# A new instruction order for an attention and feed-forward kernel: second-half K/Q loads ahead of the weights, scores of steps 2 and 3 ahead of the feed-forward part, copies split over two engines

## Chip, cores and metric

The kernel runs on one core of a Trainium2 chip. The metric is the device time of one execution in microseconds (us), lower is better. The profile's engines are TensorE (PE; PEld is its weight load), VectorE (DVE), ScalarE (ACT), GpSimd (POOL) and SyncE (SP, used here to issue transfers). "Clock" is the mean granted TensorE clock of a run, 1.0 being full speed.

## What is computed

Four batches of eight heads, 768 positions, head dimension 64. In the inputs given, three heads attend causally, the other five only to the first 4 positions and a window of 64. The result goes through a feed-forward part that takes the larger of three products.

```python
scores = np.where(mask, scale * q @ k.T, -1e9)           # mask per head: causal, or first 4 + window
a = np.exp(scores - max); a = a / a.sum(-1)
attn = a @ v                                              # (4, 8, 768, 64)
x = attn.transpose(0, 2, 1, 3).reshape(3072, 512)
h = np.maximum(np.maximum(x @ w1, x @ w2), x @ w3)        # 512 -> 768, three weights
out = h @ w_out                                           # 768 -> 512
```

## The kernel before

The work is 16 *steps* (batch, half of the sequence, quartet of heads) of attention and eight *feed-forward parts* (batch, half). A part needs the turned result xT of two steps. Its work is cut into groups, which a generator hands out one by one between the scores of later steps ("fill"), so that TensorE has something to do while ScalarE takes exponentials.

```python
def load(b, qd):                  # K and Q of four heads of a batch, cast to fp16 on the way
    st = stage.tile([P, 2, S // R, D], FP16, tag="kq", name="kq")
    for i, src in enumerate((k, q)):
        nc.gpsimd.dma_start(out=st[:, i], in_=src[b, G * qd : G * qd + G]...)
# ... cut ...
def ffn(b, half):                 # one feed-forward part, one "yield" a group
    for wi, ni in order:
        yy = psum()
        for ks in range(KS):
            nc.tensor.matmul(yy[:, 0:HALF], w_t[wi][:, ks, ...], xT[b, half][ks]..., ...)
        if wi == 0:
            nc.scalar.copy(out=acc[ni], in_=yy[:, 0:HALF])           # accumulator copy
        else:
            nc.vector.tensor_tensor(out=dst, in0=yy, in1=acc[ni], op=ALU.max)
        yield
# ... cut ...
def av(t, i):                     # attention product of a head pair, scaled, then turned
    # ... matmuls into o, x = o / row sums ...
    if t in BY_DMA:               # steps 2 and 4 to 15: turned by a transposing transfer
        nc.sync.dma_start(out=xT[b, half][hp], in_=x..., transpose=True)
    else:                         # the other steps: turned on TensorE
        xs[t, i] = x
# ... cut: the start, up to the first feed-forward groups ...
PROGRAM = (                       # due groups, whether pairs are apart, four lists of items
    # ... cut ...
    (2.8, False, "", "", "av 4 1", "av 5 0, load 2 0, v 6 0 pp"),
    (3.6, False, "x 5 0", "load 2 1", "", "av 5 1"),
    # ... cut: ten rows ...
    (3.94, False, "", "", "av 9 0, v 9 1 ap", "load 3 0"),
    (3.6, False, "", "x 9 0, load 3 1", "x 9 1", ""),
    # ... cut ...
)
```

`load b qd` loads K and Q of four heads of batch b; `turn` turns them in 32x32 blocks on VectorE; `v` casts values; `masks` (called in the scores) multiplies exponentials by the mask.

The softmax here doesn't subtract the row's maximum and nothing guards it: scores larger than these inputs give would overflow.

Of the kernel before, what the change touches and what calls it, by code (L numbers as in the profile page):

```python
# [38 lines left out]
APART = [(0, 0, 1, (384,), 128, 0), (1, 1, 1, (384,), 128, 0)] + MASKED[1][1:]  # L39

# [11 lines left out]
def kernel(  # L52
# [14 lines left out]
    nc = tc.nc  # L67
# [21 lines left out]
    BY_DMA = (2, 4, 5, 6, 7, 8, 9, 10, 11, 12, 13, 14, 15)  # L89

    consts = ctx.enter_context(tc.tile_pool(name="consts", bufs=1))
    stage = ctx.enter_context(tc.tile_pool(name="stage", bufs=3))
    half16 = ctx.enter_context(tc.tile_pool(name="half16", bufs=3))
# [27 lines left out]
    def load_pairs(half, hp, n, engines, alone=False):  # L121
        for nm, src, eng in zip(("ks", "qs"), (k, q), engines):
            st = stage.tile([P, 4, HB, D], FP32, tag=nm, name=nm)
            m = 2 if alone else 2 * n
            for h in range(0, 2 * n, m):
                eng.dma_start(
                    out=st[:, h : h + m],
                    in_=src[
                        0, 2 * hp + h : 2 * hp + h + m, half * HALF : (half + 1) * HALF
                    ].rearrange("h (p j) d -> p h j d", p=P),  # L130
                )
            for i in range(n):
                staged.setdefault((half, hp + i), []).append(st[:, 2 * i : 2 * i + 2])

# [12 lines left out]
    def turn_pair(half, hp, *engines):  # L147
# [4 lines left out]
        for part, op in enumerate(engines):  # L152
            tr = bank([P, 1024], FP16, "tr")
            for i in range(n):
                for j in range(HB):
                    c = i * HALF + j * P
                    nc.tensor.transpose(  # L157
                        tr[:, c : c + P],
                        xs[part + i][:, j].rearrange("p h d -> p (h d)"),
                        ident,  # L160
                    )
# [34 lines left out]
    after = consts.tile([1, 2], FP16, name="after")  # L196

    def sync_after(x):
        nc.sync.dma_start(out=after, in_=x)
# [3 lines left out]
    def load_v(b, half, engines=None):  # L203
        engines = engines or (nc.sync,) * HB
        vs = stage.tile([P, H, HB, D], FP32, tag="vs", name="vs")
        for j in range(HB):
            r0 = half * HALF + j * P
            engines[j].dma_start(
                out=vs[:, :, j], in_=v[b, :, r0 : r0 + P].rearrange("h p d -> p h d")
            )  # L210
        staged_v[b, half] = vs

    load_pairs(0, 0, 1, (nc.sync, nc.scalar))
    ir32 = consts.tile([1, 2 * H], mybir.dt.int32, name="ir32")
    nc.sync.dma_start(out=ir32, in_=is_retrieval.bitcast(mybir.dt.int32).unsqueeze(0))
    load_pairs(0, 1, 1, (nc.sync, nc.scalar))
    load_pairs(0, 2, 2, (nc.sync, nc.scalar), True)
    load_v(0, 0)


    zero = consts.tile([P, 512], FP16, name="zero")
    nc.vector.memset(zero, 0.0)

# [52 lines left out]
    def head_flags():  # L276
        flags = bank([P, H], FP32, "flags")
        nc.tensor.matmul(flags, base[0:1, 0:P], RT1, start=True, stop=True)
# [26 lines left out]
    def load_weight(wi):  # L305
        if wi < 3:
            nc.gpsimd.dma_start(
                out=w_t[wi],
                in_=(moe_w1, moe_w2, moe_w3)[wi].rearrange("(ks p) n -> p ks n", p=P),
            )  # L310
        else:
            nc.gpsimd.dma_start(
                out=woutt, in_=moe_w_out.rearrange("(ns p) m -> p ns m", p=P)
            )
# [4 lines left out]
    def ffn(b, half):  # L319
# [15 lines left out]
        for wi, ni in order:  # L335
            yy = psum()
            for ks in range(KS):
# [5 lines left out]
                )  # L343
            if wi == 0:
                acc[ni] = accp.tile([P, HALF], FP16, tag="acc", name="acc")
                nc.scalar.copy(out=acc[ni], in_=yy[:, 0:HALF])  # L346
# [6 lines left out]
        for tb in range(HB):  # L353
# [5 lines left out]
            for c, op, eng in (  # L359
                (0, nc.scalar.copy, nc.sync), (n, nc.vector.tensor_copy, nc.scalar),  # L360
# [14 lines left out]
    queue = []  # L375

    def fill(n):
# [28 lines left out]
    def scores(t, u, pairs=(0, 1)):  # L406
# [5 lines left out]
        m = 1 if u == 1 and (t == 0 or t == 1 and pairs == (0,)) else 2  # L412
# [37 lines left out]
        for x, st in sts.items():  # L450
# [5 lines left out]
            if not early:  # L456
                masks(t, i, u)


    MASK_ON_DVE = ((2, 0, 1), (3, 0, 0), (3, 0, 1), (3, 1, 3), (5, 0, 0), (5, 1, 0), (5, 1, 1), (7, 0, 1))  # L460

    def masks(t, i, u):
# [3 lines left out]
        for at, u0, nu, cols, n, m0 in APART if t in (3,) else MASKED[half]:  # L466
# [11 lines left out]
            engine = nc.vector if (t, i, u) in MASK_ON_DVE else nc.gpsimd  # L478
# [4 lines left out]
    def av(t, i):  # L483
# [29 lines left out]
        if t in BY_DMA:  # L513
# [6 lines left out]
    def turn_x(t, i, op=None):  # L520
        b, half, qd = where(t)
        hp = 2 * qd + i
        if t not in BY_DMA:
# [10 lines left out]
        if hp == NHP - 1:  # L534
# [4 lines left out]
    cast_pair(0, 0, (act, act))  # L539
    idle_work(8)  # L540
    read_flags()
    idle_work(2)
    head_flags()
    turn_pair(0, 0, dve, act)
    head_masks(0, True)
    cast_pair(0, 1, (pool, act))
    turn_pair(0, 1, dve)
    cast_pair(0, 2, (pool, pool))
    scores(0, 0, (0,))
    scores(0, 1, (0,))  # L550
    head_masks(1, True)
    load_weight(0)
    scores(0, 0, (1,))
    far_flags()
    cast_pair(0, 3, (pool, pool))
    head_masks(3, True)
    head_masks(2, True)
    turn_pair(0, 2, dve)
    scores(0, 1, (1,))
    turn_pair(0, 3, dve)  # L560
    prep_v(0, 0, dve, nc.gpsimd)
    prep_v(1, 0, dve, nc.vector)
    load_pairs(1, 0, 2, (nc.gpsimd, nc.gpsimd))
    prep_v(1, 1, pool, nc.gpsimd)
    scores(1, 0, (0,))
    scores(1, 1, (0,))
    scores(1, 0, (1,))
    prep_v(0, 1, act, nc.vector)
    av(0, 0)
    scores(1, 1, (1,))  # L570
    av(1, 0)
    av(0, 1)
    turn_x(0, 0, act)
    av(1, 1)
    load_weight(1)
    turn_x(0, 1, act)
    head_masks(0)
    cast_pair(1, 1, (act, act))
    load_pairs(1, 2, 2, (nc.gpsimd, nc.gpsimd))
    load_weight(2)  # L580
    load_v(0, 1, (nc.gpsimd,) * HB)
    turn_x(1, 0, dve)
    turn_x(1, 1, dve)
    cast_pair(1, 0, (act, act))
    fill(4)
    head_masks(2)
    turn_pair(1, 1, dve)
    turn_pair(1, 0, dve)
    head_masks(3)
    load_weight(3)  # L590
    fill(1)
    fill(1)
    fill(1)
    head_masks(1)






    FIRST = 4
    PROGRAM = (
        (2.4, True, "", "", "cast 1 2 dp", ""),
        (2.4, False, "load 1 0", "", "cast 1 3 da", ""),
        (2.0, False, "", "pair 1 2", "load 1 1", ""),
        (2.2, False, "pair 1 3", "v 2 0 ap", "", "v 2 1 ap"),
        (2.2, False, "", "gate, load_v 1 0", "", ""),
        (1.6, True, "", "av 2 0", "", "turn 1 0 0 0"),
        (1.0, True, "turn 1 0 0 1", "", "av 2 1, turn 1 0 1 0", ""),
        (2.2, True, "turn 1 0 1 1, load_v 1 1", "", "v 3 1 pp, v 3 0 ap, x 2 0", "turn 1 1 0 0"),  # L610
        (3.6, False, "turn 1 1 0 1", "x 2 1", "turn 1 1 1 1, av 3 1", ""),
        (2.8, False, "v 4 0 pp, av 3 0", "turn 1 1 1 0", "v 4 1 ap", ""),
        (3.6, False, "x 3 0, x 3 1", "", "", ""),
        (3.6, False, "av 4 0", "", "x 4 0, v 5 1 pp", "x 4 1, v 5 0 ap"),
        (2.8, False, "", "", "av 4 1", "av 5 0, load 2 0, v 6 0 pp"),
        (3.6, False, "x 5 0", "load 2 1", "", "av 5 1"),
        (3.8, False, "", "x 5 1", "", ""),
        (2.8, False, "", "load_v 2 0", "turn 2 0 1 0", "v 6 1 ap"),
        (4.8, False, "turn 2 0 0 1", "", "turn 2 0 0 0", "av 6 0"),
        (4.2, False, "", "", "", "x 6 0, x 6 1, turn 2 0 1 1"),  # L620
        (3.4, False, "", "av 6 1", "turn 2 1 0 1", ""),
        (5.4, False, "load_v 2 1", "v 7 0 ap, turn 2 1 0 0", "turn 2 1 1 0", "v 7 1 ap"),
        (3.4, False, "", "turn 2 1 1 1", "v 8 0 ap, x 7 0", "av 7 0"),
        (3.8, False, "av 7 1", "", "", "v 8 1 pp"),
        (3.94, False, "x 7 1", "", "av 8 0", "v 9 0 ap, av 8 1"),
        (3.2, False, "", "x 8 0, x 8 1", "", ""),
        (3.94, False, "", "", "av 9 0, v 9 1 ap", "load 3 0"),
        (3.6, False, "", "x 9 0, load 3 1", "x 9 1", ""),
        (5.6, False, "v 10 0 ap, av 9 1", "v 10 1 ap", "", ""),
        (3.14, False, "", "load_v 3 0", "turn 3 0 1 0", ""),  # L630
        (3.6, False, "turn 3 0 0 1", "av 10 0", "turn 3 0 0 0", ""),
        (3.4, False, "", "x 10 0", "av 10 1", "turn 3 0 1 1"),
        (6.2, False, "", "", "turn 3 1 0 1", "v 11 0 ap"),
        (3.2, False, "load_v 3 1", "turn 3 1 0 0", "turn 3 1 1 0", ""),
        (3.2, False, "v 11 1 pp", "x 10 1, turn 3 1 1 1", "v 12 0 ap", "av 11 0, x 11 0"),
        (3.4, False, "", "av 11 1", "", "v 12 1 ap"),
        (5.0, False, "x 11 1", "", "av 12 0", "v 13 0 ap, av 12 1"),
        (3.2, False, "", "x 12 0, x 12 1", "", ""),
        (4.0, False, "", "", "av 13 0, v 13 1 pp", ""),
        (5.2, False, "", "x 13 0", "x 13 1", ""),  # L640
# [86 lines left out]
```

## Time and profile before

| | before |
|---|---|
| time, median of the runs beside the changed kernel | 200.95 us (200.65 to 201.27, 4 runs); this kernel's runs in the later rounds had clock 0.996 to 1.0 |
| TensorE, VectorE, ScalarE, GpSimd busy | 189.7, 122.5, 131.7, 123.3 us of a span of 199.3 |
| first feed-forward matmul of parts 0, 1, 2, 3 | 17.8, 50.1, 70.9, 94.3 us |
| K/Q loads of batch 2 issued, of batch 3 issued | 56.7 and 62.9 us; 100.3 and 105.5 us |

A second measure is used below: **lost time**. I give every matmul, the idle ones at the start left out, the time that it takes at the steady pace of the same traces (0.163 us for 384 columns, 0.216 us for 512, and so on), which sums to 171.4 us for either kernel, and subtract from the clock of the span the work begun until then. Before, 17.1 us are lost at 50 us, 18.4 at 70, 19.0 at 80 and 24.1 at 190 us. It is my own sum, good to a few tenths; it also sees slow matmuls and small gaps, which the busy columns hide.

### The profile page before, as it was taken

How to read it: one execution, taken by the hardware profiler on the slowest of the kernel's cores; microseconds unless marked ns; L12 is line 12 of the kernel's file. 1: busy time of each engine (PE TensorE's matmuls, PEld its weight loads, DVE VectorE, ACT ScalarE, POOL GpSimd, SP SyncE). 2: the span in 40 equal slices, each digit the busy share in tenths (PEclk: the TensorE clock that was granted, in tenths of full speed). 3: DMA queues.
4: the chain of work that ended last, by engine and by line, in shares of the span. 5: the costliest groups of instructions: out<-in, count | busy, mean ns of one | idle time of the engine just before them, and what ended most of it. 6: DMA issues, size and time to landing. Idle time of an engine off the chain costs nothing.

```text
span 199.3 us, 5133 instructions
## 1 busy us (share of the span) xinstructions
PE 189.7 (95%) x2059; PEld 109.5 (55%) x2059; DVE 122.5 (61%) x241; ACT 131.7 (66%) x206; POOL 123.3 (62%) x154
## 2 busy tenths in 40 slices
PE   7897999996999999999999999999999999999992
PEld 2455555545566465574555565565555565755652
DVE  2698587999687829861555649961555234543540
ACT  4585798786966776676786775848758769323221
POOL 3599159789887906787969635799847447400000
PEclk9999999999999999999999999999999999999999
DMA  6999999994949991904359995513410250023004
GB/s 182 270 213 245 278 238 212 213 202 112 256 81 154 194 274 43 178 0 146 95 101 132 170 254 141 85 26 98 116 23 20 105 76 20 3 64 135 3 0 158
DMA packets 43245, 26.48 MB, mean 133 GB/s; under 512 B 33558, under 2 KB 38230, under 8 KB 43222
## 3 DMA queue, kind: packets, MB, share of 16 engines
q1 hardware_dynamic: 37206, 15.01, 34.9%
q0 software_dynamic: 4784, 10.23, 26.7%
q10 hardware_dynamic: 1232, 0.92, 1.5%
q8 instruction: 16, 0.26, 0.6%
q14 instruction: 7, 0.06, 0.1%
HBM read 25.17 MB, written 6.29 MB: 158 GB/s over the span
## 4 chain that ended last, share of the span: by engine, by line
PE 78%; DVE 8%; ACT 4%; DMA 3%; issue 3%; POOL 2%; SPq 1%; ACTq 0%; POOLq 0%; DVEq 0%
PE yy L338 43%; PE yy L364 12%; PE st L441 10%; PE oacc L495 8%; DVE KQ L190 4%; PE yst L338 3%; ACT pt L452 3%; DMA ks<-in_k_dram 2%; DVE x L505 2%; DMA out_dram<-ot 1%; PE tr L157 1%; PE yst L364 1%; POOL kn L139 1%; DVE hT L349 1%; POOL qn L139 0%
## 5 line engine op out<-in xcount | busy, mean ns | idle before, releaser
L479 POOL TENSOR_TENSOR pt<-pt,mk 128x512 f16<-128x512 f16 (+1 forms) x76 | 80.6, 1084 | 34.8 <-ACT pt L452 34.7
L452 ACT ACTIVATE pt<-st 128x1024 f16<-128x1024 f32 (+3 forms) x99 | 83.1, 894 | 19.4 <-PE st L441 18.6
L349 DVE TENSOR_TENSOR acc<-yy,acc 128x384 f16<-128x384 f32 x45 | 25.1, 558 | 28.9 <-PE yy L338 19.3
L338 PE MATMUL yy<-xT,w1t 128*128 128x384 f16 x180 | 36.1, 327 | 0.1
L338 PE MATMUL yy<-xT,w0t 128*128 128x384 f16 x180 | 35.6, 326 | 0.4 <-DVE xT L531 0.4
L338 PE MATMUL yy<-xT,w2t 128*128 128x384 f16 x180 | 35.7, 327 | 0.0
L346 ACT CAST acc<-yy 128x384 f16<-128x384 f32 x45 | 21.0, 485 | 17.0 <-PE yy L338 10.5
L364 PE MATMUL yy<-woutt,hT 128*128 128x512 f16 (+1 forms) x138 | 32.0, 375 | 0.0
L441 PE MATMUL st<-KQ 32*128 32x384 f16 (+4 forms) x560 | 28.7, 279 | 1.0 <-DVE KQ L190 0.8
L349 DVE TENSOR_TENSOR hT<-yy,acc 128x384 f16<-128x384 f32 x45 | 25.1, 560 | 6.6 <-PE yy L338 4.0
L495 PEld LDWEIGHTS <-pt 128*128 128x128 f16 x672 | 24.0, 97 | 5.3 <-issue 2.1
L190 DVE STREAM_TRANSPOSE KQ<-kq 128x384 f32<-128x384 f32 x24 | 25.7, 1130 | 0.0
L338 PEld LDWEIGHTS <-w0t 128*128 128x128 f16 x192 | 18.2, 98 | 12.9 <-issue 1.0
L495 PE MATMUL oacc<-va,pt 128*128 128x65 f16 x352 | 24.8, 193 | 0.3 <-ACT va L392 0.3
L338 PEld LDWEIGHTS <-w2t 128*128 128x128 f16 x192 | 17.6, 98 | 13.3 <-issue 2.1
L338 PEld LDWEIGHTS <-w1t 128*128 128x128 f16 x192 | 17.2, 98 | 12.8 <-issue 1.3
L370 ACT COPY ot<-yy 128x512 f32<-128x512 f32 x22 | 12.9, 588 | 15.9 <-PE yy L364 9.6
L364 PEld LDWEIGHTS <-hT 128*128 128x128 f16 x150 | 14.0, 98 | 14.6 <-issue 0.3
L441 PEld LDWEIGHTS <-KQ 32*128 32x128 f16 (+1 forms) x560 | 12.2, 93 | 17.8 <-issue 11.5
L495 PE MATMUL oacc<-vf,pt 128*128 128x65 f16 x320 | 21.2, 193 | 0.8 <-POOL vf L394 0.8
L505 DVE TENSOR_TENSOR x<-oacc,rc 128x384 f16<-128x384 f32 x32 | 17.8, 557 | 1.1
L503 DVE RECIPROCAL rc<-oacc 128x6 f32<-128x6 f32 x32 | 6.1, 192 | 20.0 <-PE oacc L495 19.8
(70 smaller groups left out, 129.9 us busy)
## 6 DMA issues: line engine op xcount, KB each, us to landing
out_dram<-ot SPq DMA_DIRECT2D x23, 256.0 KB, 3.1
vs<-in_v_dram SPq DMA_DIRECT2D x21, 256.0 KB, 6.3
kq<-in_k_dram POOLq DMA_DIRECT2D x6, 384.0 KB, 5.6
kq<-in_q_dram POOLq DMA_DIRECT2D x6, 384.0 KB, 8.0
qs<-in_q_dram ACTq DMA_DIRECT2D x4, 192.0 KB, 4.0
ks<-in_k_dram SPq DMA_DIRECT2D x4, 192.0 KB, 3.6
w0t<-in_moe_w_dram POOLq DMA_DIRECT2D x1, 768.0 KB, 7.4
ks<-in_k_dram POOLq DMA_DIRECT2D x2, 384.0 KB, 7.2
```

What stands on the lines that cost most here:

```text
L190: nc.vector.transpose(out=dst.rearrange("c (p j) -> c j p", j=n)[:, j0:j1], in_=src.rearrange("c (j i) -> c j i", i=R),)
L338: nc.tensor.matmul(yy[:, 0:HALF], w_t[wi][:, ks, ni * P : (ni + 1) * P], xT[b, half][ks].rearrange("p a t -> p (a t)"), start=(ks == 0), s ...
L346: nc.scalar.copy(out=acc[ni], in_=yy[:, 0:HALF])
L349: nc.vector.tensor_tensor(out=dst, in0=yy[:, 0:HALF], in1=acc[ni], op=ALU.max)
L364: nc.tensor.matmul(yo[:, 0:n], hT[ns][:, tb * P : (tb + 1) * P], woutt[:, ns, c : c + n], start=(ns == 0), stop=(ns == NNB - 1),)
L370: op(out=ot[:, c : c + n], in_=yo[:, 0:n])
L441: nc.tensor.matmul(sts[g // m][:, g % m, c0 : c0 + n * P], KQ[rows, 0, ki * P : (ki + 1) * P], KQ[rows, 1, t0 : t0 + n * P], start=(c0 == ...
L452: nc.scalar.activation(out=pts[t, i][:, u, h0 : h0 + m, 0:w], in_=st[:, :, 0:w], func=AF.Exp, scale=sc,)
L479: engine.tensor_tensor(out=x, in0=x, in1=m, op=ALU.mult)
L495: nc.tensor.matmul(o[:, qi, hl, 0 : D + 1], pt[:, u, hl, c : c + P], vv[:, 2 * hp + hl, ki, 0 : D + 1], start=(idx == 0), stop=(idx == len ...
L503: nc.vector.reciprocal(out=rc, in_=o[:, :, :, D])
L505: nc.vector.tensor_tensor(out=x, in0=o[:, :, :, 0:D], in1=rc.unsqueeze(3).to_broadcast([P, HB, 2, D]), op=ALU.mult,)
```

## The change

The intent: TensorE is busy 95% and its idle time lies in the first 50 us. So the second half's K and Q of batch 0 are loaded ahead of the weights and the scores of steps 2 and 3 go ahead of feed-forward part 0; the order is written out item by item; accumulator copies and masks are split over the engines, by a letter at each item (d VectorE, a ScalarE, p GpSimd). Core of the diff, long cuts marked:

```diff
+PROGRAM = (
+    "cast 0 0 pp, idle 8, read, flags, turnp 0 0 aa, em 0, cast 0 2 pp, cast 0 1 pd, s 0 0 0",
+    "ld 1 0, turnp 0 2 dd, far, em 2, cast 0 3 aa, s 0 1 0 b, turnp 0 1 ad, em 3, ld 1 2",
+    "turnp 0 3 aa, em 1, s 1 0 0, s 1 0 1, s 0 0 1, w 0, s 0 1 1, s 1 1 0 b, cast 1 0 dp",
+    # ... cut ...
+    "v 4 0 ap, load 2 0, f 1 a, f 1 d, f 1 d, f 1 d, s 5 1, v 5 0 ap, k 4 0 1 d, f 1 d",
+    "v 4 1 ap, k 4 1 1 p, k 5 1 1 d, k 4 0 0 p, k 5 0 1 p, load 2 1, k 5 0 0 p, av 4 0 D, f 1 a",
+    "s 6 0, f 1 d, f 1 a, av 4 1 D, f 1 a, s 6 1, k 5 1 0 d, v 5 1 pp, f 1 a, av 5 0 D",
+    "av 5 1 D, f 1 d, k 6 1 1 p, s 6 2, f 1 d, load 3 0, f 1 a, f 1 a, f 1 a, s 6 3, k 6 0 1 p",
+    # ... cut ...
+    "f 1 a, f 1 a, load 3 1, x 7 1 a, f 1 d, turn 3 0 0 1, turn 3 0 1 0, k 9 0 1 p, f 1 a",
+    # ... cut ...
+)
-                nc.scalar.copy(out=acc[ni], in_=yy[:, 0:HALF])
+                copy_out[0](out=acc[ni], in_=yy[:, 0:HALF])
-    MASK_ON_DVE = ((2, 0, 1), (3, 0, 0), (3, 0, 1), (3, 1, 3), (5, 0, 0), ...)
-    def masks(t, i, u):
+    def masks(t, i, u, engine):
-    cast_pair(0, 0, (act, act))
-    idle_work(8)
-    # ... the whole start, the old PROGRAM and its slots: cut ...
+    for line in PROGRAM:
+        for item in line.split(", "):
+            name, *args = item.split()
+            do[name](*args)
```

In the list, `s` is scores, `k` masks, `f` a feed-forward group and the engine of its copy, `av ... D` a product whose x is turned by a transfer, `ld` and `load` K/Q loads, `w` weights, `idle` matmuls on zeros that are meant to keep the clock up at the start.

## The prediction

> **What bounds the kernel now.** I read the page's engine totals and its strips of 40 slices (about 5 us each) first.
>
> ```profile
> span 199.3 us, 5133 instructions
> ...
> PE 189.7 (95%) x2059; PEld 109.5 (55%) x2059; DVE 122.5 (61%) x241; ACT 131.7 (66%) x206; POOL 123.3 (62%) x154
> ...
> PE   7897999996999999999999999999999999999992
> ...
> DMA  6999999994949991904359995513410250023004
> ```
>
> TensorE is busy 95%, and the slices below 9 lie in the first 50 us and the last slice. DMA is near full only in the first 45 us. So the question is not what the change saves on average, but what it does to the first 50 us. The window sums say the same with numbers (columns: stretch, its length, busy us of each engine, granted clock, DMA share, GB/s):
>
> ```profile
> 5.60:18.60 13.00, 10.89 (x136) 6.92 (x136) 11.82 (x32) 8.80 (x17) 11.34 (x19) 1.00 1.17 243
> 18.60:34.00 15.40, 15.22 (x123) 8.33 (x123) 11.97 (x25) 12.42 (x21) 9.07 (x12) 1.00 1.14 241
> 34.00:50.00 16.00, 13.70 (x214) 8.09 (x212) 14.89 (x24) 12.52 (x17) 14.02 (x17) 1.00 0.85 176
> 50.00:104.00 54.00, 54.00 (x641) 31.68 (x630) 35.18 (x66) 39.75 (x61) 39.47 (x49) 1.00 0.69 138
> 104.00:150.00 46.00, 45.90 (x537) 26.63 (x539) 27.77 (x51) 32.42 (x52) 33.19 (x38) 1.00 0.63 116
> 150.00:195.70 45.70, 45.69 (x424) 26.52 (x416) 19.08 (x38) 23.47 (x38) 14.44 (x14) 1.00 0.20 52
> ```
>
> From 50 us to the last matmul TensorE is idle 0.11 us of 145.7: a new order can't win there, only lose. Idle is 2.11 us at 5.6 to 18.6, 0.18 at 18.6 to 34 and 2.30 at 34 to 50, together 4.6. In the last of these VectorE is 93% busy. What TensorE waits for (total us, times, longest), from the waits view:
>
> ```profile
> PE tr L527 <- DVE x L505: 1.2, 3, 0.6
> PE st L441 <- DVE KQ L190: 0.8, 2, 0.5
> PE oacc L495 <- POOL vf L394: 0.8, 1, 0.8
> PE tr L157 <- ACT qn L139: 0.7, 1, 0.7
> PE yy L338 <- DVE xT L531: 0.4, 1, 0.4
> ```
>
> Never long for one engine: early, casts and copies come late; at 44 to 50 us, the scaled values (vf), the x tiles and the 32x32 transposes of the second batch's K and Q (L190). Last, the transfers, as issue time on GpSimd plus time to landing, against the first use of the output weights:
>
> ```profile
> 19.99 0.83 POOL L312 DMA_DIRECT2D woutt<-in_moe_w_out_dram  x1
> ...
> 37.23 1.46 PE L364 MATMUL yy<-woutt,hT 128*128 128x512 f16 x6
> ```
>
> ```profile
> w0t<-in_moe_w_dram POOLq DMA_DIRECT2D x1, 768.0 KB, 7.4
> ...
> w1t<-in_moe_w_dram POOLq DMA_DIRECT2D x1, 768.0 KB, 9.1
> ...
> woutt<-in_moe_w_out_dram POOLq DMA_DIRECT2D x1, 768.0 KB, 17.2
> ```
>
> The output weights land at 19.99 + 17.2 = 37.2 and are used at 37.23: the old order runs just behind the transfers. By the same sum w0 (issued 8.13) lands at 15.5, w1 (14.27) at 23.4, w2 (16.55 + 12.7) at 29.3.
>
> **What the Trainium skill says.** "DMA: Bandwidth & Descriptors", section Rules for kernel authors: transfers from SP, ACT and GpSimd share the same 16 DMA engines, so spreading them adds no bandwidth. The trace agrees: share 1.14 to 1.17 while two kinds of queue are active. Putting K/Q first therefore puts the weights later by the same bytes. "Perfetto Trace Analysis", section Optimization Strategy: where a kernel has several regimes, interleaving them can help. That is this change: attention without weights fills the regime bound by transfers. Same page, section Optimizing Scalar/DVE Operations: GpSimd and VectorE share an SBUF read port, so moving work between them may not help. The trace of before agrees in part: ten masks on VectorE have a median of 0.585 us, but one took 2.31 us at 34.9 us, when GpSimd was at work on the same kind of tensors.
>
> **The change part by part.** The order of instructions against before shows the same 2,060 matmuls and as many weight loads, so nothing is removed from TensorE.
>
> 1. *Start.* Ten idle matmuls, 427 ns apart, end at 5.5 us and the first real transpose starts at 5.75. Now eight come first and two later, and the flag matmul no longer needs the mask constant: transposes can start when the first casts are ready. Those casts move to GpSimd; the inputs land at 4.05 and 4.4 us, and two casts of 0.5 us end at about 5.1. Start earlier by 0.5 us, minus 0.43 for the two idle matmuls put back: about 0.
>
> 2. *5 to 16 us.* The first scores no longer stand behind the transpose of pair 1, which waited 0.7 us for a ScalarE cast. The first scores start near 6.1 instead of 7.7 us (my addition of durations). But ScalarE then limits: the early exponentials are four of 1.02, four of 0.6 (or pairs of 0.38), about 7 us, plus casts and five copies of 0.48 us that now lie on ScalarE between them. Added up they end near 15.6 us, as before (15.9). I expect 0 to 1 us.
>
> 3. *Second-half K/Q ahead of the weights.* Two pairs of transfers (3.1 MB read) now go before w0 (1.6 MB read, landed in 4.1 us per piece in mid-stretch). K/Q should land at about 15 and 18 us, w0 at 21 to 22, w1 near 25.5, w2 near 32. Meanwhile TensorE can do scores of steps 2 and 3: about 16 score groups of 0.17 to 0.27 us, 3.9 us in all, and four half-0 products of 0.37 us. Feed forward then starts near 22 us instead of 17.8 us, with w0 just there, but with the exponentials of steps 2 and 3 running 6 us earlier.
>
> 4. *34 to 50 us.* Attention of the first batch is done before its feed forward is, so the second feed-forward part (18 groups of 0.65 and three of 1.30, 15.6 us) is ready as filler while K/Q of the second batch is turned. From 22 us to the first scores of step 5 I add 26.9 us of work: 11.7 feed-forward groups, 3.9 output groups, 3.3 of the next part, 2.7 remaining scores, 3.8 half-1 products, 0.9 scores of step 4, 0.6 transposes. That gives 49 to 50 us without stall, 51 with 1 to 2 us of stall; the old order has the same work done at about 52.8 us (its step-5 scores at 49.51, then the five groups of the next part). Gain 1.5 to 3.5 us.
>
> 5. *Copies and masks split.* 23 of 48 accumulator copies and six output copies go from ScalarE to VectorE, and masks go from 10 on VectorE and 76 on GpSimd to 43 and 43. VectorE gains 33 x about 0.5 = 17, 23 x 0.55 = 13, 6 x 0.6 = 4, some 7 for value scaling, less 5 for K/Q copies given up: about 36 us, to some 158 us (80%). ScalarE falls to about 118 and GpSimd to about 90 us. No engine passes TensorE, so from 50 us on this is worth nothing by itself.
>
> 6. *End.* 3.6 us from the last matmul to the end; same code, same eight fill steps ahead of the last part. 0.
>
> Sum: 0 + 0.5 + 2.5 + 0.2 (the one wait at 104 to 150) = 3.2 us, so 201.25 - 3.2 = 198.0.
>
> **Rivals.** *(a) Nearly all stalls go.* Idle is 4.6 us, and the gaps that lie hidden under the overlap of matmul records add perhaps 3 more: 194 to 196 us. For it: an order this irregular looks searched, and the new filler is large. Against: ScalarE limits the start. *(b) A new wait for weights or the second batch's K/Q.* Their issues stand in GpSimd's queue behind masks that wait for exponentials: the output weights are issued only after a mask of step 3, about 35 us, and K/Q of heads 4 to 7 at about 41 instead of 32 us; landing 5 to 8 us later is just in time. If late, 1 to 3 us go back: 199 to 201. *(c) VectorE becomes the bound.* In 12 to 48 us my sum of its work leaves little free, and in the steady part it goes from 60% to perhaps 85%, with masks that can stretch from 0.6 to over 2 us when GpSimd is at the same port. If TensorE waits 0.3 us once per 10 us after 50 us, that is 4 us: 201 to 203.
>
> **Range and chances.** The floor is near 194 (no stall), the loss cases end near 202. Centre 198.0, 8 in 10 within 195.2 to 201.3. Faster by over 2% needs under 197.2, which takes most of the first 50 us' stalls: 0.37. Within 2%: 0.57. Slower: 0.06.
>
> **What would show each step.** Step 2: first exponential near 6.7 instead of 8.6 us, yet the last early one still near 15.6. Step 3: first w0 matmul at 21 to 23 us, no wait for it over 0.5 us. Step 4: TensorE idle in 34 to 50 us under 1 us; first scores of step 5 near 50 us after five groups of the second feed-forward part. Step 5: VectorE near 158, ScalarE near 118, GpSimd near 90 us, and idle after 50 us still under 1 us. The prediction is wrong if the weights are waited for by several us, if VectorE's load puts new waits after 50 us, or if the start is better than ScalarE's sum allows.

## More of the kernel before

Columns: stretch, its length, busy us and instruction count of PE, PEld, DVE, ACT and POOL, then granted clock, DMA share and GB/s.

```profile
50.00:70.00 20.00, 20.00 (x226) 11.30 (x215) 15.56 (x28) 15.17 (x23) 16.96 (x22) 1.00 0.98 172
70.00:80.00 10.00, 10.00 (x138) 6.14 (x137) 6.18 (x13) 7.03 (x11) 3.43 (x3) 1.00 0.71 161
80.00:95.00 15.00, 15.00 (x177) 8.96 (x176) 8.41 (x17) 10.34 (x17) 11.95 (x15) 1.00 0.44 103
95.00:110.00 15.00, 14.90 (x167) 8.55 (x166) 8.20 (x18) 11.40 (x20) 13.13 (x18) 1.00 0.66 114
```

TensorE is busy without a break; VectorE has over 6 us free in each 15 us; the DMA share is near 1 between 50 and 70 us, and lower after that. K/Q loads of batch 2 are issued at 56.7 and 62.9 us, of batch 3 at 100.3 and 105.5 us.

## The result

The changed kernel took 205.93 us (median; 203.33 to 207.67, 4 runs) against 200.95 us before. Its fast runs over those of before give 1.0142, interval 1.0099 to 1.0186. Ratios here are the mean time of one kernel's fast runs over the mean of the other's fast runs of the same rounds, so not quite the ratio of the medians quoted. The time lies above the predicted range, and the kernel became slower, by less than 2% but clear of the noise. Two of its four runs (203.33 and 204.42 us, clock 0.999 and 0.998) count as fast; the other two (207.43 and 207.67 us) had clock 0.983 and 0.975. The profile is of a slow one, so its clock must be read with it. A half-clock record of 3.41 us (shown below) takes 0.83% off the mean clock of a span of 205 us: 0.983 stands for two such records, 0.975 for three, and 0.998 or 0.999 for none. So the fast runs, which were not profiled, lost their 1.42%, some 2.9 us, without any half-clock record. First the page of the changed kernel: span, TensorE's totals and strips of 40 slices.

```profile
span 205.4 us, 5121 instructions
PE 191.5 (93%) x2059; PEld 109.8 (53%) x2059; DVE 154.1 (75%) x319; ACT 114.3 (56%) x166; POOL 87.2 (42%) x121
...
PE   7797799889999949999999999999999999999993
...
PEclk9799999999999987999999999999999999999999
DMA  6999995799999999411698652121320040114004
```

One dent in TensorE's strip is new and deep, from 72 to 77 us (slices are 5.1 us, so this is the fifteenth); small ones lie at 21 to 26 and 36 to 46 us, and the dent of before at 45 to 50 us is gone. The clock strip has two dents, in the second slice and from 72 to 82 us. DMA is near full without a break from 41 to 82 us; before, there were gaps at 45 to 50, 55 to 60 and 75 to 80 us. Windows of the changed kernel, with the stretches of the prediction:

```profile
5.60:18.60 13.00, 11.17 (x124) 7.03 (x123) 10.37 (x22) 11.28 (x22) 9.98 (x19) 0.87 1.17 271
18.60:34.00 15.40, 13.68 (x127) 7.58 (x125) 13.61 (x36) 12.87 (x18) 9.27 (x12) 1.00 1.09 213
34.00:50.00 16.00, 14.36 (x203) 8.89 (x201) 14.00 (x27) 6.67 (x10) 9.65 (x11) 1.00 0.92 122
50.00:104.00 54.00, 50.74 (x593) 27.89 (x590) 45.04 (x83) 34.47 (x51) 30.23 (x42) 0.97 0.87 160
```

TensorE's idle time up to 50 us is 1.83 + 1.72 + 1.64 = 5.2 us, where it was 2.11 + 0.18 + 2.30 = 4.6: what was gained at 34 to 50 us was lost at 18.6 to 34. From 50 to 104 us it is 3.26 us where it was none. The same stretch of the changed kernel in the finer windows shown for before:

```profile
50.00:70.00 20.00, 19.93 (x218) 10.88 (x215) 16.95 (x33) 14.56 (x23) 14.62 (x22) 1.00 1.25 211
70.00:80.00 10.00, 7.26 (x58) 3.28 (x56) 5.87 (x9) 4.41 (x8) 2.27 (x2) 0.83 1.12 231
80.00:95.00 15.00, 15.00 (x230) 9.48 (x227) 13.29 (x31) 9.58 (x14) 5.92 (x9) 1.00 0.35 72
95.00:110.00 15.00, 14.22 (x154) 7.52 (x151) 14.46 (x23) 9.44 (x13) 8.62 (x11) 1.00 0.86 163
```

From 70 to 80 us TensorE is idle 2.74 us and its clock is 0.83. In the last two rows VectorE is 89% and 96% busy. The waits view of the changed kernel (total us, times, longest):

```profile
PE yy L437 <- DMA xT<-x: 2.7, 1, 2.7
...
PE tr L633 <- DVE x L611: 1.1, 2, 0.7
PE tr L230 <- POOL kn L211: 0.9, 1, 0.9
PE oacc L601 <- POOL pt L585: 0.9, 1, 0.9
PE yy L473 <- DMA woutt<-in_moe_w_out_dram: 0.8, 1, 0.8
```

The largest is one wait of a feed-forward product for xT that a transfer turns. Four lines of timelines of the changed kernel (start, duration, engine and line, what; in brackets the wait before it) tell how it comes about. Of SPq's line the duration covers four transposes one after the other.

```profile
60.15 8.90 SPq L620 DMA_TRANSPOSE xT<-x  x4
...
65.76 0.59 POOL L250 DMA_DIRECT2D kq<-in_k_dram  x1
66.35 0.54 POOL L250 DMA_DIRECT2D kq<-in_q_dram  x1
...
75.02 0.32 PE L437 MATMUL yy<-xT,w0t 128*128 128x384 f16 x1 [2.74 <-DMA xT<-x]
```

The fourth transpose is issued at 65.94 us and lands at 74.97 (the last of its 16 completion counts), after 9.0 us, of which SyncE's issue takes 3.1. Just ahead of it stands the K/Q load of batch 3, heads 0 to 3. In the kernel before the same load is issued 35 us later:

```profile
100.27 0.59 POOL L174 DMA_DIRECT2D kq<-in_k_dram  x1
```

There too, two transposes issued behind that load and the next, at 101.25 and 106.41 us, take 8.1 us, but the part that needs them starts only at 116.5 us. Transposes with no K/Q load in flight mostly land 2.3 to 2.4 us after issue, as 16 of the 26 of the kernel before do. "DMA: Bandwidth & Descriptors", section Queues, rings and completion order, of the Trainium skill says that each DMA engine takes turns between queues, and that a completion count lands only after every earlier write of that engine, across its queues. The trace fits this: the K load lands at 73.98, the Q load at 76.06 and the transpose between them. I cannot tell the two mechanisms apart with these runs.

By lost time, the kernels compare so (us lost up to the mark):

| at | 50 | 70 | 80 | 95 | 190 |
|---|---|---|---|---|---|
| before | 17.1 | 18.4 | 19.0 | 19.6 | 24.1 |
| changed | 17.4 | 18.8 | 23.8 | 24.9 | 30.1 |
| difference | 0.3 | 0.5 | 4.8 | 5.3 | 6.0 |

In the profiled, slow run the first 50 us gave nothing, 70 to 80 us cost 4.3 us, and 80 to 190 us another 1.2. Of the 4.3, 2.74 are the wait. The rest is the clock. The clock records of the trace give half speed for 3.41 us from 7.55 us and for 3.41 us from 75.81 us; half of 3.41 is 1.7. The matmuls bear the second one out: four of 384 columns take 1.48 us at 77.11 us, and 0.82 at 79.40. The kernel before has one record at full speed from 7.18 to 198.33 us, a microsecond before the end. "TensorE: Matmul & The Clock Gate", Part 1 (What's actually happening), states a free-running activity window of 3413 ns with half rate after an idle one. The length agrees with the records.

The early window explains little of the first 50 us. At 15 us the changed kernel and run 4 below, which has no early window, have lost the same, and at 18 us they agree within 0.1 us. They part after that, at a pair of multiplications by which VectorE scales values. The changed kernel first, then run 4:

```profile
15.46 2.91 DVE L505 TENSOR_TENSOR vf<-vs,far 128x128 f16<-128x128 f32 x2
```

```profile
15.35 1.58 DVE L505 TENSOR_TENSOR vf<-vs,far 128x128 f16<-128x128 f32 x2
```

Behind the longer pair stand, on VectorE, the copy of turned K/Q and the x tiles, and TensorE waits for both:

```profile
19.29 0.39 PE L552 MATMUL st<-KQ 64*128 64x384 f16 x4 [0.62 <-DVE KQ L238]
...
21.14 0.34 PE L633 MATMUL tr<-ident,x 128*128 128x128 f16 x3 [0.66 <-DVE x L611]
```

So part 0 starts at 23.3 us instead of 22.1. The pair takes 2.91 us in eight of the profiles of the new order (the changed kernel's and those of runs 1, 2, 3, 5, 6, 12 and 14) and 1.5 to 1.6 in three (4, 10 and 11), with casts on GpSimd beside it in all; why it takes the one or the other is not known.

### The profile page after: what moved, and what is told of

The parts are those of the page before. It is cut to its first block, busy times and chain, and to the rows that moved or that the text cites. A ratio compares the mean times of both kernels' runs of the same rounds, so it can differ in the third digit from the quotient of the medians.

```text
span 205.4 us, 5121 instructions
## 1 busy us (share of the span) xinstructions
PE 191.5 (93%) x2059; PEld 109.8 (53%) x2059; DVE 154.1 (75%) x319; ACT 114.3 (56%) x166; POOL 87.2 (42%) x121
## 4 chain that ended last, share of the span: by engine, by line
PE 72%; DMA 13%; DVE 9%; issue 3%; POOL 1%; SPq 1%; DVEq 0%
PE yy L437 41%; PE yy L473 9%; PE st L552 8%; DMA xT<-x 8%; PE oacc L601 8%; DMA ks<-in_k_dram 5%; DVE KQ L266 3%; PE yst L437 3%; DVE vf L505 1%; DVE x L611 1%; PE yst L473 1%; DVE hT L457 1%; DVE kn L211 1%; POOL kn L211 0%; DVE KQ L238 0%
## 5 line engine op out<-in xcount | busy, mean ns | idle before, releaser
L585 POOL TENSOR_TENSOR pt<-pt,mk 128x512 f16<-128x512 f16 (+1 forms) x43 | 46.8, 1108 | 47.3 <-ACT pt L563 45.4
L437 PE MATMUL yy<-xT,w0t 128*128 128x384 f16 x180 | 36.6, 331 | 3.2 <-DMA xT<-x 2.7
L437 PE MATMUL yy<-xT,w2t 128*128 128x384 f16 x180 | 36.5, 331 | 0.4 <-DVE x L611 0.4
L552 PE MATMUL st<-KQ 32*128 32x384 f16 (+5 forms) x560 | 29.0, 282 | 1.1 <-DVE KQ L238 0.6
L457 DVE TENSOR_TENSOR hT<-yy,acc 128x384 f16<-128x384 f32 x45 | 24.9, 554 | 3.8 <-PE yy L437 1.8
L266 DVE STREAM_TRANSPOSE KQ<-kq 128x384 f32<-128x384 f32 x24 | 25.1, 1137 | 0.0
L585 DVE TENSOR_TENSOR pt<-pt,mk 128x512 f16<-128x512 f16 (+1 forms) x43 | 22.6, 547 | 1.4 <-ACT pt L563 1.4
L479 ACT COPY ot<-yy 128x512 f32<-128x512 f32 x16 | 9.4, 588 | 21.3 <-PE yy L473 20.4
L454 ACT CAST acc<-yy 128x384 f16<-128x384 f32 x24 | 11.6, 488 | 14.0 <-PE yy L437 12.4
```

The source lines that it names most:

```text
L266: nc.vector.transpose(out=dst.rearrange("c (p j) -> c j p", j=n)[:, j0:j1], in_=src.rearrange("c (j i) -> c j i", i=R),)
L437: nc.tensor.matmul(yy[:, 0:HALF], w_t[wi][:, ks, ni * P : (ni + 1) * P], xT[b, half][ks].rearrange("p a t -> p (a t)"), start=(ks == 0), s ...
L454: copy_out[0](out=acc[ni], in_=yy[:, 0:HALF])
L457: nc.vector.tensor_tensor(out=dst, in0=yy[:, 0:HALF], in1=acc[ni], op=ALU.max)
L479: op(out=ot[:, c : c + n], in_=yo[:, 0:n])
L552: nc.tensor.matmul(sts[g // m][:, g % m, c0 : c0 + n * P], KQ[rows, 0, ki * P : (ki + 1) * P], KQ[rows, 1, t0 : t0 + n * P], start=(c0 == ...
```

## The experiments

**Theory A.** The load of batch 3 was pulled ahead to 65.76 us and holds up the transposing transfer that part 2 needs at 72 us; the stall then makes the clock fall. **Theory B.** The time is lost at the start, to a thin clock window and to late weights. **Theory C.** VectorE's added copies and masks are the loss. (The expectations call A "T" or "T2" and C "V"; the "Theory C" in that of run 4 is the clock.) Unless stated, the edit is made in the changed kernel, and before's runs on the same chips were 200.2 to 202.3 us.

### 1. The load alone moved later

```diff
-    "... s 6 2, f 1 d, load 3 0, f 1 a ..."
+    "... s 6 2, f 1 d, f 1 a ..."
-    "... k 7 1 1 p, f 1 d ..."
+    "... k 7 1 1 p, load 3 0, f 1 d ..."
```

> The changed kernel with one move: the K/Q load of batch 3, heads 0 to 3, is issued some 16 us later (near 82 us on GpSimd instead of 65.8). Theory T (the loss after 50 us is TensorE waiting for the DMA transpose of step 5, which stands behind that load): the wait of 2.7 us at 72 us falls under 0.3 us, fast runs near 201.0 (203.3 to 204.4 less 2.7), and the half-clock window at 76 us is gone, so slow runs are rarer. Rival V (VectorE's added work is the loss, the DMA wait only shows it): the wait at 72 us turns into one on VectorE or the loss after 80 us grows, time 203 to 204.

Measured: 207.59 us (204.36 to 207.85, 6 runs), ratio 1.0221 (1.0165 to 1.0278). The wait at 72 us is gone: the last transpose, issued at 65.21, lands after 5.1 us instead of 9.0, and lost time at 80 us is 18.8 us, that of before. But the load, now issued at 77.47, did the same to another transfer. The values of batch 2 came late, ScalarE stood at their cast, and the feed-forward copy stood behind that cast. Timelines of this run, first ScalarE, then TensorE:

```profile
86.13 0.51 ACT L503 CAST va<-vs 128x384 f16<-128x384 f32 x1 [3.61 <-DMA vs<-in_v_dram]
...
87.08 1.44 PE L437 MATMUL yy<-xT,w0t 128*128 128x384 f16 x4 [2.83 <-ACT acc L454]
```

Two half-clock windows followed from 86.25 us. So A's cause is shown for the wait at 72 us: none of the seven profiles with this load moved (runs 1, 5, 6, 9, 11, 12 and 14) has it, and those with the load in place and step 5 turned by transfer (the changed kernel, runs 3, 4, 8 and 10) have 1.8 to 2.8 us of it. My expected gain was a miss: the new place was bad.

### 2. Step 5 turned on TensorE instead of by transfer

```diff
-    "... av 5 0 D", "av 5 1 D, f 1 d ..."
+    "... av 5 0", "av 5 1, f 1 d ..."
-    "... x 5 1 d, turn 2 0 1 0 ..."
+    "... x 5 0 a, x 5 1 d, turn 2 0 1 0 ..."
```

> The changed kernel, load left early, but the x tiles of step 5 are turned on TensorE instead of by DMA. Theory T: TensorE no longer needs the DMA there, wait gone for 0.4 us of extra transposes and two extra copies, fast runs near 201.3. Rival V: if the x tiles themselves were late (VectorE), the wait stays as one on DVE x, 203 to 204.

Measured: 205.22 us (204.31 to 206.11, 4 runs), ratio 1.0198, a miss. The wait was exchanged: 1.6 us for ScalarE's copy of xT, 1.4 us for VectorE's combinations, 1.1 us for the transfers of step 4 that remain. Three of four runs had clock 1.0. Shorter waits left the clock alone, but the sum of time stayed.

### 3. Output weights loaded earlier

```diff
-    "... av 2 0 D, w 3, f 1 a ..."
+    "... av 2 0 D, f 1 a ..."
-    "... load 1 0, v 2 0 dp ..."
+    "... load 1 0, w 3, v 2 0 dp ..."
```

> The changed kernel with the output weights issued right after the first K/Q load of batch 1 (near 29 instead of 35.7 us). Theory: they land near 40 instead of 45.2 us, the 0.8 us wait at 44.3 us goes, and the second K/Q load of batch 1 is not later, so fast runs gain 0.5 to 0.9: 202.6 to 203.5. Rival (what is saved there is given back at the next wait, the K/Q of batch 1 or the DMA at 72 us): under 0.2 us gained.

Measured: 205.2 us (203.48 to 207.72, 4 runs), ratio 1.018. The 0.8 us wait for the output weights is gone, and the scores wait 0.6 us for VectorE at 43.1 us instead. Lost time at 50 us, 18.0 us, includes a wait of 1.6 us for turned K/Q and a half-clock window at 22.9 us. The wait for xT is 2.1 us here, and no half-clock window follows it. Inconclusive, and too small to be the cause.

### 4. Ten idle matmuls at the start

```diff
-    "cast 0 0 pp, idle 8, ..."   /   "... s 1 1 1, idle 2, turnp 1 0 aa ..."
+    "cast 0 0 pp, idle 10, ..."  /   "... s 1 1 1, turnp 1 0 aa ..."
```

> The changed kernel with ten idle matmuls at the start and none at 16 us, as in the kernel before. Theory C (slow runs of the changed kernel are half-clock windows of 3.4 us, one after the thin start, one after the stall at 72 us, each costing about 1.7 us): the window near 7.6 us goes in most runs; slow runs are then near 205.7 instead of 207.5 and fast runs stay 203.3 to 204.4. Rival (the state is the chip's and has nothing to do with the start): slow runs near 207.5 as often as without the edit.

Measured: 205.88 us (203.1 to 207.58, 6 runs), ratio 1.0164. In the profiled run no half-clock window came before 70 us, and lost time at 50 us was 15.4 us, 1.65 less than before. **This is the gain that the change was made for, but it stands in this one profile.** The missing window is not what made it: runs 2, 6 and 14 have no window in the first 50 us either, and their profiles have lost 17.5, 17.0 and 17.7 us at 50 us. What run 4 has is the short pair of multiplications shown above, and no wait for the output weights (0.8 us in the changed kernel). The lead was given back at 70.0 us by a wait of 2.8 us for xT and the window behind it. Over the six runs times go with clock: 1.0 gave 203.1 us, 0.998 gave 204.63, 0.992 gave 205.19 and 206.58, 0.99 gave 207.0, 0.983 gave 207.58.

### 5 and 6. The load after the last values of step 11, without and with ten idle matmuls

```diff
-    "... s 6 2, f 1 d, load 3 0, f 1 a ..."
+    "... s 6 2, f 1 d, f 1 a ..."
-    "... v 11 0 ap, k 7 0 2 p ..."
+    "... v 11 0 ap, load 3 0, k 7 0 2 p ..."
```

> The changed kernel with the K/Q load of batch 3, heads 0 to 3, issued only after the values of batch 2 have landed (GpSimd reaches it a few us after 80). The first move of this load (to 77.5 us) took away the DMA wait at 72 us, but the load then stood ahead of the last value load and made a wait of 2.8 us at 84 us. Theory T2 (this load has no room between 59 and 80 us, whatever stands behind it waits): now neither wait is there, the lost time between 70 and 95 us falls from 6.0 (changed) to under 2.0 us, no half-clock window after 70 us, time 200.3 to 201.5. Rival V (VectorE is what is short): a wait of 2 us or more on a VectorE copy or mask comes in its place, time over 202.5.

> The same move, and ten idle matmuls at the start. The run with ten idle matmuls and nothing else had the second feed-forward part begin at 47.8 us against 50.1 in the kernel before, in a run without a half-clock window before 70 us. If the lead at 50 us is real and T2 holds, this is 199.3 to 200.6, under the kernel before (200.9), with no slow runs. Rival: the lead at 50 us is given back after 80 us to VectorE, 200.9 or more.

Measured: 204.43 us (202.83 to 207.42, 6 runs), ratio 1.0157; with the idle matmuls 204.11 us (202.1 to 208.34, 6 runs), ratio 1.0105 (1.0058 to 1.0151). Both expected times were missed. In run 5 there is no wait at 72 or 84 us; at 95 us lost time is 20.7 us, against 24.9 in the changed kernel and 19.6 before. Now the *next* load of batch 3 met the transposes of part 3: issued at 93.87 and 94.46 us, it landed at 98.9 (K) and 101.5 (Q), and a transpose issued just before it, at 93.00, landed between them, at 100.43. TensorE in run 5:

```profile
100.47 0.49 PE L437 MATMUL yy<-xT,w0t 128*128 128x384 f16 x2 [3.68 <-DMA xT<-x]
```

A half-clock window starts at 100.82 us. Run 6 has the same wait, of 4.3 us, with a half-clock record of 6.83 us from 99.09 us. So in these runs the wait came whether the load fell a little before a transpose that was soon needed or a little after it.

### 7. The same fault put into the kernel before

```diff
-        (2.8, False, "", "", "av 4 1", "av 5 0, load 2 0, v 6 0 pp"),
-        (3.6, False, "x 5 0", "load 2 1", "", "av 5 1"),
+        (2.8, False, "", "", "av 4 1", "av 5 0, load 2 0, load 2 1, load 3 0, v 6 0 pp"),
+        (3.6, False, "x 5 0", "", "", "av 5 1"),
-        (3.94, False, "", "", "av 9 0, v 9 1 ap", "load 3 0"),
+        (3.94, False, "", "", "av 9 0, v 9 1 ap", ""),
```

> The kernel before with one thing of the change: the K/Q loads of batch 2 and of batch 3, heads 0 to 3, issued one after another from 57 us on (in the kernel before 56.7, 62.9 and 100.3 us). Theory T2: in the old order too TensorE then waits for a DMA transpose or for values, 1.5 to 4 us near 71 us or later, time 202.5 to 205, perhaps with a half-clock window. Rival (the wait comes from the new order or split, not from the load): within 0.7 us of the kernel before.

Measured: 202.51 us (201.92 to 203.15, 4 runs), ratio 1.0075 (1.0045 to 1.0106), and a wait that the kernel before does not have:

```profile
PE yy L338 <- DMA xT<-x: 1.6, 2, 1.3
```

Transposes issued at 58.4, 60.0 and 63.7 us landed at 70.5, 72.7 and 73.3, around the last of the six K/Q transfers (72.4). The edit pulls two loads: batch 3's first by 41 us and batch 2's second by 5 us. So K/Q loads pulled together make the wait without any other part of the change; which of the two does it is not told apart here. No wait was long enough here for a half-clock window (clock 0.996 to 1.0).

### 8. First weight ahead of the second-half K/Q

```diff
-    "ld 1 0, turnp 0 2 dd, ..."   /   "... s 0 0 1, w 0, s 0 1 1 ..."
+    "w 0, ld 1 0, turnp 0 2 dd, ..."   /   "... s 0 0 1, s 0 1 1 ..."
```

> The changed kernel with w0 loaded ahead of the second-half K/Q, as in the kernel before. If loading K/Q first is what makes the early scores possible: K/Q land about 4 us later, TensorE waits some 3 to 4 us at 16 to 20 us and the lead at 50 us is gone; lost time at 50 us 19 to 21 us instead of 17.4, and fast runs at 205 to 207. If it does not matter: within 0.7 us of the changed kernel's 203.3 to 204.6.

Measured: 210.45 us (209.32 to 211.82, 4 runs), ratio 1.0472. TensorE waits 3.9 us for the cast K of the second half, which lands late:

```profile
PE tr L230 <- DVE kn L211: 3.9, 1, 3.9
```

Lost time at 50 us is 22.4 us, more than expected and 5.0 more than in the changed kernel; a half-clock record of 6.83 us from 17.89 us is 3.4 of it. With these early scores K/Q must come first: that part of the change did what it should. And as the changed kernel nowhere waits for w0, w1 or w2, theory B in its form "the weights come too late" is left with the 0.8 us for the output weights.

### 9. Both loads moved, ten idle matmuls

```diff
 (edits of 4 and 5, and)
-    "f 1 a, f 1 a, load 3 1, x 7 1 a ..."
+    "f 1 a, f 1 a, x 7 1 a ..."
-    "... k 9 1 1 p, f 1 d, f 1 d, f 1 d ..."
+    "... k 9 1 1 p, load 3 1, f 1 d, f 1 d, f 1 d ..."
```

> The changed kernel with three edits: the K/Q load of batch 3's heads 0 to 3 after the last V piece of step 11 (as in the run that moved it there), the load of heads 4 to 7 of batch 3 moved behind a later mask, and ten idle matmuls at the start. Theory (transposes by transfer that wait behind K/Q loads, and the half-clock windows that follow such stalls and the thin start): the waits of TensorE for xT near 72, 84 and 96 us are all gone or under 1 us, no half-clock window in the profiled run, lost time at 50 us near 15.5 us and under 21 at 100 us, and the fast runs at 199.5 to 201.5 us, so a ratio to before of 0.992 to 1.003. Rival (VectorE's added copies and masks are what the new order loses by): the lost time still grows by over 3 us more than before's between 80 and 196 us, and the fast runs stay above 202.5 us. Second rival: the moved load shifts the wait to yet another place (the K/Q turns of batch 3), seen as a wait of over 2 us for kq or KQ after 105 us.

Measured: 203.5 us (202.07 to 242.74, 6 runs), ratio of the fast runs 1.0095 (1.0067 to 1.0123). Four of six runs were 202.07 to 203.57 us. The run of 242.74 us, which is the profiled one, had a granted clock of 0.75 from 6 us to the end; its waits for xT are gone, but its times say nothing, and I have no explanation for that clock. The expected 199.5 to 201.5 us was a miss: 1.9 us more than before (0.95% of 201) remain.

### 10. All feed-forward copies on ScalarE again

```diff
-    f 1 d                      (every one)
+    f 1 a
```

> The changed kernel with all copies of the feed-forward part on ScalarE again, as in the kernel before: 29 copies go from VectorE to ScalarE, nothing else. Theory (transfers and clock): the wait for xT at 72 us stays within 1 us of the 2.7 us of the changed kernel, so the time stays within 1.5 us of it, 203 to 207 us. Rival (VectorE is short): VectorE's busy time falls by some 15 us to near 139, the small waits for VectorE at 98 to 110 us go, and the time falls by 2 us or more, to 202 or less in the fast runs. If instead the copies on ScalarE hold up the exponentials, waits for pt before oacc appear between 20 and 50 us and lost time at 50 us is over 18 us.

Measured: 203.79 us (202.69 to 205.12, 4 runs), ratio 1.0143 (1.0107 to 1.0179). The wait for xT is still there, somewhat shorter, and this time no half-clock window follows it:

```profile
73.36 0.32 PE L437 MATMUL yy<-xT,w0t 128*128 128x384 f16 x1 [1.78 <-DMA xT<-x]
```

VectorE's busy time falls to 136.8 us. Lost time from 80 to 190 us is 5.0 us: 6.3 in the changed kernel, 5.1 before. So theory C fits the 1.2 us after 80 us, by one profile on each side, and not the 4.3 us before. The time does not show it: the ratio is the changed kernel's, and all four runs have a clock of 0.983 to 0.992, one to two half-clock windows.

### 11. Run 9 with two masks back on GpSimd

In the changed kernel two masks of steps 8 and 9 stand on VectorE while GpSimd is at masks too, and take 3.5 us together (mean of all masks on VectorE: 0.55 us each). VectorE's timeline in the changed kernel:

```profile
98.29 3.51 DVE L585 TENSOR_TENSOR pt<-pt,mk 128x512 f16<-128x512 f16 x2
```

The 0.44 and 0.34 us for which TensorE waits at 102.5 and 106.3 us are for the VectorE work behind them. This is what "Perfetto Trace Analysis" (Optimizing Scalar/DVE Operations) leads one to expect of two engines with a shared port.

```diff
-    "... s 9 0, k 8 0 1 d ..."   /   "... k 9 0 0 d, s 9 1 ..."
+    "... s 9 0, k 8 0 1 p ..."   /   "... k 9 0 0 p, s 9 1 ..."
```

> The first kernel of this call with two masks (steps 8 and 9, at about 95 to 100 us) put back from VectorE to GpSimd; in the changed kernel that pair of VectorE masks took 3.5 us beside GpSimd's own. If those stretched masks are what costs after 80 us, lost time between 90 and 110 us falls by 0.4 to 1.2 us against the first kernel of this call and the fast runs come out 0.3 to 1.2 us lower, near 199.5 us. If not, the two agree within 0.3%, and masks on GpSimd may come late for the products instead: a wait for pt from GpSimd before oacc at 98 to 104 us.

(The "first kernel of this call" is that of run 9.)

Measured: 202.27 us (201.48 to 203.06, 6 runs), ratio 1.0067 (1.0043 to 1.0091). All six runs are fast, with clock 0.996 to 1.0, and the profile has no wait for xT at all. By fast runs the loss falls from 1.42% to 0.67%, about half; the medians fall by 3.7 of 5 us because no slow runs come any more, where two of four were slow. How much of this the masks did is not shown: the intervals of runs 9 and 11 overlap. Lost time is 17.0 us at 50 us (1.7 of it a late cast of K at 9 us), 19.0 at 80, 21.1 at 95 and 25.2 at 190: level with before until 80 us, then 1.5 us behind by 95 us, and after that it falls no further behind (4.2 us against 4.5).

### 12. Run 11 with the copies on ScalarE

The edit of run 10 on top of run 11.

> The version with both loads moved, ten idle matmuls and two masks on GpSimd again, and now all copies of the feed-forward part on ScalarE as in the kernel before. If VectorE's added copies are what the rest is lost to (6.25 us lost between 80 and 196 us, against 5.1 before), that loss falls to 5.0 to 5.3 us and the fast runs come out about 1.2 us lower, at 200.3 to 201.6 us, level with before or up to 0.5% faster. If the rest is in the order of turns and scores, not in the copies, the loss after 80 us stays over 6 us and the time stays at 202 us.

Measured: 202.4 us (201.21 to 204.34, 6 runs), ratio 1.0049 (1.0019 to 1.0079). Lost time from 80 to 190 us is 6.3 us, as in run 11. The copies brought nothing here: a miss for C as I had put it. By stretch, 80 to 95 and 95 to 190 us:

| lost us | before | changed | 10 copies | 11 masks | 12 both | 14 (below) |
|---|---|---|---|---|---|---|
| 80 to 95 | 0.6 | 1.1 | 1.1 | 2.1 | 2.0 | 1.3 |
| 95 to 190 | 4.5 | 5.3 | 4.0 | 4.2 | 4.3 | 6.1 |

After 95 us the added loss goes when *either* the copies *or* the two masks leave VectorE. That looks like a pile-up at one place, 98 to 106 us, and not a steady lack; it rests on one profile of each kernel.

### 13. The split of copies alone, in the kernel before

```diff
-                nc.scalar.copy(out=acc[ni], in_=yy[:, 0:HALF])
+                (nc.vector.tensor_copy if ni % 2 else nc.scalar.copy)(out=acc[ni], ...)
```

> One part of the change alone, in the kernel before: every second accumulator copy (24 of 48) on VectorE instead of ScalarE, all else as it was. Prediction on record held such a split for worth nothing by itself. If VectorE is short only together with the other work that the new order gives it (33 masks more), this stays within 0.3% of before, 200.4 to 201.6 us. If a copy on VectorE costs TensorE by itself, by standing in line ahead of the combination of the next product, the time rises by 0.8 us or more, to 201.8 or above.

Measured: 201.48 us (201.29 to 201.84, 6 runs), ratio 1.0031 (1.0012 to 1.005), within the first expectation and at its edge. In the old order, with VectorE at 133.5 us, the split alone costs about 0.3%; the traces' lost times agree within 0.2 us and do not say where.

### 14. Both loads moved, ten idle matmuls, copies on ScalarE, masks left on VectorE

The edits of runs 9 and 10 together.

> The changed kernel with both K/Q loads of batch 3 moved back, ten idle matmuls at the start, and all feed-forward copies on ScalarE, but with the two masks of steps 8 and 9 left on VectorE as the changed kernel has them. The profiles of the two versions with those masks on GpSimd lost 2.0 us between 80 and 95 us, those with the masks on VectorE 1.1 to 1.4 us. If the masks on GpSimd cost that, lost time between 80 and 95 us is under 1.5 us here, between 95 and 196 us near 4.0 us, and the fast runs come out at 200.5 to 201.8 us. If the moved load costs it, the loss between 80 and 95 us stays near 2 us and the time near 202.3 us.

Measured: 203.76 us (201.09 to 205.28, 6 runs), ratio 1.0092 (1.0044 to 1.0141). At 80 to 95 us 1.3 us are lost, which points at the two masks on GpSimd as the 0.7 us or so that runs 11 and 12 lose more there. But the time is a miss, for a wait that I had not expected: VectorE stands at a cast of values of batch 3, whose transfers were issued at 97.9 to 99.4 us, right behind the moved K/Q load (96.8 and 97.4), and TensorE waits 1.24 us for VectorE's combination behind it. VectorE's timeline in this run:

```profile
108.66 0.60 DVE L503 CAST va<-vs 128x384 f16<-128x384 f32 x1 [2.43 <-DMA vs<-in_v_dram]
```

It looks like the mechanism of run 1 once more. No version beat the kernel before; the best of the new order, runs 11 and 12, are 0.7% and 0.5% slower by their fast runs, and do not differ beyond their intervals.

## Why the prediction was wrong

**What bounds the kernel** was right: TensorE, 93% to 95% in either kernel. The reading "DMA is near full only in the first 45 us" was wrong: the strip that it shows has nines again at 50 to 55, 60 to 75, 80 to 85 and 105 to 120 us, and the windows above give a share of 0.98 from 50 to 70 us, the very stretch into which the load was pulled. The sentence drawn from it, "From 50 us to the last matmul TensorE is idle 0.11 us of 145.7: a new order can't win there, only lose", was right too in its warning, **and then step 5 and the sum did not use it**. The step that failed most is step 5's "so from 50 us on this is worth nothing by itself" with "idle after 50 us still under 1 us": the sum counted only a gain of 0.2 us after 50 us. The profiles put there 4.3 us between 70 and 80 us (2.74 of wait, the rest a half-clock window) and 1.2 us after it. Step 4 failed too: its 2.5 us, most of the forecast gain, are not there (below). I had added up the engines' busy time and not followed a single transfer of batches 2 and 3 to its new place, although the old order's margin could be read from the trace of before: its last transpose for part 2 landed at 70.22 us, and the part's fourth matmul, the first to read what it turned, began at 71.36, 1.1 us later. Run 7 shows that K/Q loads pulled ahead, with nothing else changed, make that margin a wait in the old order; run 1, and six profiles after it, that moving the load away ends the wait in the new order.

**Step 1, start, "about 0"**: about right. The profiled run has a half-clock window from 7.55 us, but by 18 us run 4, without one, has lost no less. Nothing in the prediction spoke of the clock, while half-clock windows are, by the clocks, what the slow runs of this kernel have and the fast ones have not.

**Step 2, early scores**: the first scores start at 6.18 instead of 8.16 us, yet the last early exponential ends at 16.02 (15.92 before), as the ScalarE limit in the prediction had it. Lost time at 15 us is 10.0 us, 9.2 before: minus 0.8 us where 0 to 1 were expected.

**Step 3, K/Q first**: part 0 starts at 23.3 us against "near 22 us"; w0 landed at 20.8, no wait for w0, w1 or w2. Right for the loads, and run 8 shows that their order was needed; but TensorE is idle for 1.72 us from 18.6 to 34 us, where it was 0.18. Of this, 1.1 us is more than in run 4 and goes with the long pair of value scalings on VectorE, work that step 5 had counted only as busy time. (The share of 1.14 to 1.17, read there as agreeing with the skill on shared DMA engines, is in keeping with it but tests nothing.)

**Step 4, gain of 1.5 to 3.5 us by 50 us**: measured minus 0.3 us in the profiled run, and 1.65 us in run 4 alone. In its own stretch, 34 to 50 us, the new order does lose 1.8 us less than the old, with 1.64 us idle where under 1 was forecast; but 2.1 us more were lost by 34 us. Run 4, with the short pair of multiplications, reached the lower end; run 11 had it too, and lost the lead to a cast of K that came 1.7 us late.

**Step 5, engine sums**: VectorE 154.1 us (predicted 158), ScalarE 114.3 (118), GpSimd 87.2 (90). Right. That no engine passes TensorE did not make it harmless: rival (c) came true in small, 1.2 us after 80 us, and in the stretch from 12 to 48 us, for which it had said that little would be left free.

**Step 6, end**: no difference, right. **Rivals**: (b) came true with 0.8 us for the output weights. The rival that decided it, a transfer pulled ahead that delays a small urgent one, was not on the list.

**Still open**: the last 0.7% of run 11. Until 80 us it is level with before; 1.5 us are then lost between 80 and 95 us, of which the masks on GpSimd seem to be about half. Whether other places for the loads would win is not shown; the first two that I tried made another wait, the third made one in run 14 but not in runs 11 and 12. Why some runs get a half-clock window in the first 25 us and others of the same kernel none is not known: with ten idle matmuls at the start the profiles of runs 4 and 11 have none, that of run 12 has one at 21.05 us.

## What to carry to other kernels

When an order changes, list every transfer with its issue, landing and first use before and after, and look for a bulk load that moved ahead of a small transfer with little slack; engine totals do not show it. Here a stall of 2.7 us on TensorE cost 1.7 us more through the clock, so look at the clock records before explaining a spread. When copies are split by engine totals, look also whether a single stretch of the receiving engine fills up, as VectorE's did at 13 to 22 us and, it seems, at 98 to 106 us.

## What the Trainium skill lacked or had wrong

- "DMA: Bandwidth & Descriptors", DMA Transpose (X-bar), has constraints and alternatives but no time for a small transpose, alone or beside loads. Here one of 128 x 384 took 2.3 us from issue to landing alone, 9.0 us in the changed kernel and 12.7 us in run 7 with K/Q loads in flight.
- "TensorE: Matmul & The Clock Gate", HAM oscillation, warns of idle gaps over about 3.4 us. Here waits of 2.74 us (changed) and 2.83 us (runs 1 and 4) were followed by a half-clock record of 3.41 or 6.83 us, while waits of 2.1 us (runs 3 and 8) and 1.78 us (run 10) were not; the limit in these runs is lower.
- The same page has states of half, full and 13/16 of the clock, and mentions one stuck at a quarter. One run of run 9's kernel stood at 0.75 from end to end, on one core, and took 242.74 us instead of 202 to 205.
- "Perfetto Trace Analysis", Optimizing Scalar/DVE Operations, says that moving work between GpSimd and VectorE might not help, but not how much it can cost ("SBUF — State Buffer", Who interferes with whom, tells who blocks whom and gives two ratios, but no time for such a pair): a pair of masks took 3.51 us on VectorE beside GpSimd's masks, where the mean of one is 0.55 us, and a pair of value scalings 2.91 us in eight profiles and 1.5 to 1.6 in three.
